# Layer 2's first product as a 2x2 block product with seven block products, its weight sums made in layer 1

## The chip, the cores and the metric

The kernel runs on one core of a Trainium2 chip. The metric is the device time of one execution in microseconds (us); lower is better. TensorE multiplies (PE in the profile, PEld its weight loads), VectorE (DVE) and ScalarE (ACT) work on elements, GpSimd (POOL) does little here, and SyncE (SP) issues the transfers.

## What is computed

An attention whose keys and values are averaged over groups of eight, then two feed-forward layers over the same 4608 tokens:

```python
k_p, v_p = k.reshape(B, H, Sp, 8, D).mean(axis=3), v.reshape(B, H, Sp, 8, D).mean(axis=3)
x = softmax(q @ k_p.T / sqrt(D)) @ v_p        # 4608 tokens x 512
h = x @ w_in;  x = (h - tanh(h)) @ w_out      # layer 1, 512 -> 2048 -> 512
h = x @ w_in2; x = (h * cos(h)) @ w_out2      # layer 2, the same sizes
```

All values are float32. The weights of both layers arrive as 64-bit numbers and are converted on the chip.

## The kernel before

The 4608 tokens are cut into 9 blocks of 512, the 2048 hidden columns into 16 tiles f of 128. TensorE works on tiles of type F32R, and each factor is kept as a high part and a low part (the rest after rounding), so one product is three matmuls: high by high, high by low, low by high. The attention of a later block runs between the steps of layer 1 on an earlier one.

A step (i, f) of layer 2 (the loop at the end of the kernel, lines 990 to 1008) has four stages:

- `emit_h2` (L763): 4 pieces of the inner dimension x 3 = 12 matmuls of 512 columns sum up h, a PSUM bank, with the weight tile `wi2[f]` loaded as the stationary side and the token block `xh`, `xl` streamed.
- `g2_a` (L773) on ACT finds the number of whole turns in h (L777, L778); DVE takes them away and clips (L780, L781, L782). `g2_b` (L785) takes the absolute value and the sine on ACT (L788, L789) and multiplies by h on DVE (L790).
- `g_second` (L597) splits the result into `gh` on ACT (L600) and `gl` on DVE (L601).
- `emit_out2` (L793): 4 x 3 = 12 matmuls of 512 columns add into the four banks `acc`, which stay open over the 16 steps of a block; `evac2` (L801) then copies them out and stores them.

All weight tiles of layer 2 stay in SBUF. They come in during block 8 of layer 1 (`w2_resident`, L734). The tokens of the next block are loaded and split one piece at a time (`x1_next`, L757). PSUM has eight banks: four `acc`, two for h, two for the attention (`att`).

The weights of layer 2 are converted in blocks 1 to 6 of layer 1: `converter` (L140) makes one float32 tile of a 64-bit one in three operations (L159 on ACT, L168 and L170 on DVE), then its high part on ACT (L174) and low part on DVE (L164) in one staging buffer `w2st`, which is stored to `s2i` or `s2o` (L677). The loop of layer 1 takes as many of its ticks after each step as a goal says (L981).

Up to block 7 of layer 1 a scheduler sets the order of the instructions on each engine. From block 8 on (`MANUAL = 8`) they stand in the order in which the code issues them. Each engine runs its own queue in order and waits on semaphores for the others.

Of the kernel before, what the change touches and what calls it, by code (L numbers as in the profile page):

```python
# [34 lines left out]
LOOK = 4  # L35


@with_exitstack
def fused_kernel(ctx: ExitStack, tc: tile.TileContext, q, k, v, w1i, w1o, w2i, w2o, out):
# [41 lines left out]
    xh = [cp.tile([128, RING], F32R, name=f"xh{c}") for c in range(KC)]  # L81
    xl = [cp.tile([128, RING], F32R, name=f"xl{c}") for c in range(KC)]
# [5 lines left out]
    s2i = [dram.tile([128, KC * 2 * 128], F32, name=f"s2i{f}") for f in range(NF)]  # L88
# [591 lines left out]
    w2_conv = converter(w2_pieces, w2_raw, w2_dest, lambda n: w2_load(n + 2), w2_fin, lambda n: True)  # L680
# [65 lines left out]
    def x1_load(i, c):
        xr = cp.tile([128, BLK], F32, tag="xe", name="xr", bufs=4)
        nc.sync.dma_start(out=xr, in_=x1s[i][:, c, :])
        xraw[i, c] = xr

    def x1_split(i, c):
        o = xoff(i)
        xr = xraw.pop((i, c))
        nc.scalar.activation(out=xh[c][:, o:o + BLK], in_=xr, func=AF.Copy)
        nc.vector.tensor_tensor(xl[c][:, o:o + BLK], xr, xh[c][:, o:o + BLK].bitcast(F32), op=ALU.subtract)

    def x1_next(i, f):  # L757
        if f % 3 == 0 and f > 0 and f <= 3 * KC:
            x1_load(i, f // 3 - 1)
        if f % 3 == 2 and f > 2 and f <= 3 * KC + 2:  # L760
            x1_split(i, f // 3 - 1)

    def emit_h2(wi, i):  # L763
        o = xoff(i)
        h = ps_h.tile([128, BLK], F32, tag="h", name="h")
        n = 0
        for c in range(KC):
            for wsel, xt in ((0, xh[c]), (0, xl[c]), (1, xh[c])):
                nc.tensor.matmul(out=h, lhsT=wi[:, c, wsel, :], rhs=xt[:, o:o + BLK], start=(n == 0), stop=(n == 3 * KC - 1))  # L769
                n += 1  # L770
        return h

    def g2_a(h, cols):  # L773
        kk = cp.tile([128, BLK], F32, tag="t0", name="kk", bufs=2)
        r = cp.tile([128, BLK], F32, tag="t1", name="r")
        for a, e in cols:
            nc.scalar.activation(out=kk[:, a:e], in_=h[:, a:e], func=AF.Identity, bias=bias_r, scale=INV_2PI)  # L777
            nc.scalar.activation(out=kk[:, a:e], in_=kk[:, a:e], func=AF.Copy, bias=-MAGIC)  # L778
        for a, e in cols:
            nc.vector.scalar_tensor_tensor(r[:, a:e], kk[:, a:e], -PI2_HI, h[:, a:e], op0=ALU.mult, op1=ALU.add)  # L780
            nc.vector.scalar_tensor_tensor(r[:, a:e], kk[:, a:e], -PI2_LO, r[:, a:e], op0=ALU.mult, op1=ALU.add)  # L781
            nc.vector.tensor_scalar(r[:, a:e], r[:, a:e], -PI_MAX, PI_MAX, op0=ALU.max, op1=ALU.min)  # L782
        return r

    def g2_b(h, r, cols):  # L785
        co = cp.tile([128, BLK], F32, tag="t4", name="co", bufs=2)
        for a, e in cols:
            nc.scalar.activation(out=r[:, a:e], in_=r[:, a:e], func=AF.Abs)  # L788
            nc.scalar.activation(out=co[:, a:e], in_=r[:, a:e], func=AF.Sin, bias=bias_c, scale=-1.0)  # L789
            nc.vector.tensor_tensor(co[:, a:e], co[:, a:e], h[:, a:e], op=ALU.mult)  # L790
        return co

    def emit_out2(wo, g, f):  # L793
        gh, gl = g
        for t in range(4):
            for n, (gt, wsel) in enumerate(((gh, 0), (gh, 1), (gl, 0))):
                nc.tensor.matmul(  # L797
                    out=acc[t], lhsT=gt[:, t * 128:(t + 1) * 128], rhs=wo[:, wsel, :],
                    start=(f == 0 and n == 0), stop=(f == NF - 1 and n == 2))
# [11 lines left out]
    if True:  # L811
# [178 lines left out]
        for i in range(NB):  # L990
            for f in range(NF):
                h = emit_h2(wi2[f], i)
                final = i == NB - 1 and f == NF - 1
                if final:
                    do_second()
# [45 lines left out]
```

## Time and profile before

| | us |
|---|---|
| median of 3 runs | 1763.99 (1760.97 to 1764.25) |
| profiled execution, its own time | 1759.05 |
| its span in the profile | 1757.2 |
| busy TensorE, DVE, ACT | 1727.4, 1291.0, 1160.6 |
| first and last h matmul of layer 2 start at | 962.9 and 1743.4 |

The span runs from the first to the last instruction of the profile. Busy times overlap, and each is a share of the whole span, over stages with different limits. The durations of matmuls overlap too, as one starts before the one ahead of it has ended; how fast they follow each other is read from their starts.

### The profile page before, as it was taken

To read this page: it belongs to the slowest core of one execution; us is meant where nothing else is said; L and a number is where in the kernel's file an instruction comes from. 1 tells how busy PE (TensorE), PEld (TensorE's weight loads), DVE (VectorE), ACT (ScalarE), POOL (GpSimd) and SP (SyncE) were. 2 spreads that over 40 slices of the span, in tenths; PEclk is the share of its full clock that TensorE was granted. 3 is DMA by queue.
4 is the path that set the end of the run, shared out by engine and by line. 5 is a ranking of instruction groups with operands and counts; after the bars stand their busy time and mean duration, and the time that the engine had idled before them with its cause. 6 is when DMAs were issued, how large, how long until landed. Compare 5 with 4: busy or idle time off the path is not lost.

```text
span 1757.2 us, 22513 instructions
## 1 busy us (share of the span) xinstructions
PE 1727.4 (98%) x7980; PEld 1421.3 (81%) x7980; DVE 1291.0 (73%) x2433; ACT 1160.6 (66%) x2081; POOL 13.8 (1%) x30
## 2 busy tenths in 40 slices
PE   6989999999999999999999999999999999999998
PEld 5767888888888888888888888888888888888887
DVE  7999999879889898877666566666666666656555
ACT  4777767677677777666565666666666666666665
POOL 2000000000000000000000000000000000000000
PEclk9999999999999999999999999999999999999999
DMA  7566756665565655423386201010101010101000
GB/s 245 192 211 210 238 179 207 196 194 181 163 207 179 202 173 163 141 78 120 130 302 208 92 1 48 1 49 1 49 0 49 1 49 0 49 1 48 1 25 24
DMA packets 116400, 202.27 MB, mean 115 GB/s; under 512 B 45376, under 2 KB 61760, under 8 KB 116288
## 3 DMA queue, kind: packets, MB, share of 16 engines
q1 hardware_dynamic: 112128, 199.79, 34.5%
q10 hardware_dynamic: 4160, 1.05, 0.3%
q8 instruction: 63, 1.03, 0.2%
q14 instruction: 49, 0.40, 0.1%
HBM read 156.76 MB, written 44.04 MB: 114 GB/s over the span
## 4 chain that ended last, share of the span: by engine, by line
PE 93%; DVE 2%; ACT 2%; DMA 1%; issue 1%; SPq 0%; ACTq 0%; DVEq 0%
PE h L769 22%; PE acc L797 22%; PE h L571 21%; PE acc L608 21%; PE att L414 2%; PE att L352 2%; PE att L381 1%; DMA raw<-in_moe_w_in_dram 1%; PE att L336 1%; DMA kv<-in_k_dram 1%; PE att L391 0%; ACT gh L600 0%; DVE w L594 0%; DMA raw<-in_moe_w_out_dram 0%; PE acc L414 0%
## 5 line engine op out<-in xcount | busy, mean ns | idle before, releaser
L769 PE MATMUL h<-xh,wi 128*128 128x512 f32 x1008 | 330.8, 389 | 0.0
L797 PE MATMUL acc<-wo,gh 128*128 128x512 f32 x1008 | 310.3, 389 | 0.0
L780 DVE SCALAR_TENSOR_TENSOR r<-kk,h 128x512 f32<-128x512 f32 (+1 forms) x145 | 99.2, 684 | 181.9 <-ACT kk L778 181.5
L797 PEld LDWEIGHTS acc<-wo,gh 128*128 128x128 f32 x1008 | 189.2, 188 | 39.2
L769 PEld LDWEIGHTS h<-xh,wi 128*128 128x128 f32 x1008 | 189.1, 188 | 39.2
L788 ACT ACTIVATE r<-r 128x512 f32<-128x512 f32 (+1 forms) x145 | 91.3, 630 | 194.9 <-DVE r L782 194.9
L571 PE MATMUL h<-xh,wi 128*128 128x512 f32 x576 | 196.5, 401 | 0.3 <-DVE wi L164 0.3
L769 PE MATMUL h<-xl,wi 128*128 128x512 f32 x504 | 196.1, 389 | 0.0
L797 PE MATMUL acc<-wo,gl 128*128 128x512 f32 x504 | 196.1, 389 | 0.0
L571 PE MATMUL h<-xh,ri 128*128 128x512 f32 x576 | 195.5, 399 | 0.0
L790 DVE TENSOR_TENSOR co<-co,h 128x512 f32<-128x512 f32 (+1 forms) x145 | 99.2, 684 | 117.7 <-ACT co L789 117.7
L608 PE MATMUL acc<-gh,wo 128*128 128x512 f32 x576 | 178.8, 393 | 6.1 <-ACT gh L600 6.1
L608 PE MATMUL acc<-gh,ro 128*128 128x512 f32 x576 | 178.3, 391 | 2.0 <-ACT gh L600 1.9
L589 DVE SCALAR_TENSOR_TENSOR w<-u,h 128x512 f32<-128x512 f32 x144 | 98.5, 684 | 97.6 <-ACT th L583 97.0
L777 ACT ACTIVATE kk<-h,bias_r 128x512 f32<-128x512 f32 (+1 forms) x145 | 99.5, 686 | 91.8 <-PE h L769 91.8
L582 ACT ACTIVATE u<-h 128x512 f32<-128x512 f32 x144 | 86.0, 597 | 92.3 <-PE h L571 91.0
L600 ACT ACTIVATE gh<-w 128x512 fp32r<-128x512 f32 x144 | 90.8, 631 | 62.7 <-DVE w L594 60.4
L608 PEld LDWEIGHTS acc<-gh,wo 128*128 128x128 f32 x576 | 107.8, 188 | 29.9 <-ACT gh L600 7.7
L608 PEld LDWEIGHTS acc<-gh,ro 128*128 128x128 f32 x576 | 107.6, 188 | 25.3 <-ACT gh L600 2.9
L571 PEld LDWEIGHTS h<-xh,wi 128*128 128x128 f32 x576 | 108.2, 189 | 22.6 <-DVE wi L164 0.7
L571 PEld LDWEIGHTS h<-xh,ri 128*128 128x128 f32 x576 | 108.2, 188 | 21.4 <-issue 0.2
L592 ACT ACTIVATE u<-u,bias_m 128x512 f32<-128x512 f32 x144 | 104.2, 724 | 30.8 <-DVE w L589 30.4
(178 smaller groups left out, 3340.8 us busy)
## 6 DMA issues: line engine op xcount, KB each, us to landing
ri<-s1i SPq DMA_DIRECT2D x64, 512.0 KB, 3.7
ro<-s1o SPq DMA_DIRECT2D x64, 512.0 KB, 3.6
raw<-in_moe_w_in_dram SPq DMA_DIRECT2D x32, 512.0 KB, 3.9
raw<-in_moe_w_out_dram SPq DMA_DIRECT2D x32, 512.0 KB, 3.5
x1s<-xe SPq DMA_DIRECT2D x36, 256.0 KB, 4.7
xr<-x1s SPq DMA_DIRECT2D x36, 256.0 KB, 4.0
out_dram<-xe SPq DMA_DIRECT2D x36, 256.0 KB, 2.0
kv<-in_k_dram SPq DMA_DIRECT2D x32, 256.0 KB, 3.8
```

The costliest lines, as they stand in the source:

```text
L571: nc.tensor.matmul(out=h[:, off:off + m], lhsT=wi[:, c, wsel, :], rhs=xt[:, r:r + m], start=(n == 0), stop=(n == 3 * KC - 1))
L582: nc.scalar.activation(out=u, in_=h, func=AF.Square)
L589: nc.vector.scalar_tensor_tensor(w, u, C2, h, op0=ALU.mult, op1=ALU.mult)
L592: nc.scalar.activation(out=u, in_=u, func=AF.Relu, bias=bias_m)
L600: nc.scalar.activation(out=gh[:, a:e], in_=w[:, a:e], func=AF.Copy)
L608: nc.tensor.matmul(out=acc[d], lhsT=wo[:, wsel, d * 128:(d + 1) * 128], rhs=gt, start=(f == 0 and n == 0), stop=(f == NF - 1 and n == 2))
L769: nc.tensor.matmul(out=h, lhsT=wi[:, c, wsel, :], rhs=xt[:, o:o + BLK], start=(n == 0), stop=(n == 3 * KC - 1))
L777: nc.scalar.activation(out=kk[:, a:e], in_=h[:, a:e], func=AF.Identity, bias=bias_r, scale=INV_2PI)
L780: nc.vector.scalar_tensor_tensor(r[:, a:e], kk[:, a:e], -PI2_HI, h[:, a:e], op0=ALU.mult, op1=ALU.add)
L788: nc.scalar.activation(out=r[:, a:e], in_=r[:, a:e], func=AF.Abs)
L790: nc.vector.tensor_tensor(co[:, a:e], co[:, a:e], h[:, a:e], op=ALU.mult)
L797: nc.tensor.matmul(out=acc[t], lhsT=gt[:, t * 128:(t + 1) * 128], rhs=wo[:, wsel, :], start=(f == 0 and n == 0), stop=(f == NF - 1 and n = ...
```

## The change

The first product of layer 2 now takes two weight tiles at a time, a pair j = f // 2, and is cut into 2x2 blocks: the inner dimension into two halves, the two tiles into one each, the 512 tokens into two halves of 256. Instead of eight block products there are seven (`product`, in the order `ORD`), each of 2 pieces x 3 = 6 matmuls of 256 columns: 42 per pair, where there were 24 of 512. Their factors are blocks or sums of blocks:

- The sums of weight blocks (four per pair of tiles) are made by the converter in layer 1 (`w2_converter`, which takes the place of `converter` there), with seven high and low parts per pair in place of the two tiles' own. `W2_TICKS` is 224 where there were 96 ticks.
- The sums of token blocks (four per token block, `sums`) and their high and low parts (seven, `fill_hi`, `fill_lo`) are made one token block ahead, spread over its 8 pairs by `WORK`. Twelve slots lie in the former `xh`, `xl`.
- The sums of the products (seven block sums) are made from PSUM: ACT copies product 1 (`hold`), DVE makes `join_a` (the first 256 tokens' two tiles, A) and `join_b` (the other half, B). Products 2 and 4 share one bank.

A and B are then handled as h was, 512 columns each, in the same operations (`turns`, `reduce`, `cosine`, `product_w`, `split`, `split_low`), and `unit` makes the second product, 12 matmuls of 512 columns each, for the two `acc` banks of its token half. A step of the loop in `second` holds the products of pair n, half A of pair n-1, and half B of pairs n-1 and n-2.

The block weights no longer stay in SBUF: for 7 of the 8 pairs their seven tiles of 256 KB are loaded anew for each token block into a ring of `WS = 18` slots (`load_slot`, one load behind each product, 441 in all); pair 7's stay. The tiles of the second product stay as before. Block 8 of layer 1 issues the first loads and the token sums of block 0 (`ahead`).

```diff
+ORD = (1, 2, 6, 7, 4, 5, 3)
...
-    w2_pieces = [(f, s) for f in range(NF) for s in range(2)]
+    w2_pieces = [(2 * j + e, s) for j in range(NF // 2) for s in range(2) for e in range(2)]
...
+    def w2_converter():
...
+            (a11, a12), (a21, a22) = [[x[:, 0:256], x[:, 256:512]] for x in (first, a)]
+            for src, sums_, ks in (
+                    (first, (), (0, 1)), (a, ((a21, a11, a21, ALU.subtract),), (3, 4)),
+                    (a, ((a21, a22, a21, ALU.subtract), (a22, a21, a11, ALU.add)), (2, 5)),
+                    (a12, ((a12, a12, a21, ALU.subtract),), (6,))):
+                for o, x, y, how in sums_:
+                    nc.vector.tensor_tensor(o, x, y, op=how)
+                    yield
+                m = len(ks)
+                st = ap.tile([128, 2, 2, 256], F32R, tag="w2st", name="w2st")
+                x = src.rearrange("p (e n) -> p e n", e=m)
+                nc.scalar.activation(out=st[:, 0:m, 0, :], in_=x, func=AF.Copy)
+                yield
+                nc.vector.tensor_tensor(st[:, 0:m, 1, :], x, st[:, 0:m, 0, :].bitcast(F32), op=ALU.subtract)
...
+    W2_TICKS = (NF // 2) * (4 * 3 + 2 * 2 + 4 * 2 + 4)
...
+    def sums(w):
+        o, x, y, how = {
+            1: ("t1", "12", "11", ALU.subtract), 3: ("12", "22", "12", ALU.subtract),
+            2: ("11", "12", "11", ALU.add), 4: ("t4", "21", "11", ALU.subtract)}[w]
+        nc.vector.tensor_tensor(raw_x(o), raw_x(x), raw_x(y), op=how)
...
+    WORK = {1: ((), (1,)), 2: ((), (3,)), 3: ((0,), (2,)), 4: ((1,), ()), 5: ((2,), (4,)), 6: ((3,), ()), 7: ((4, 5), ())}
...
+            t = two["bp"].tile([128, 2, 2, 128], F32R, tag="ws", name="ws", bufs=WS)
+            nc.sync.dma_start(out=t.rearrange("p w c n -> p (w c n)").bitcast(F32), in_=s2i[j][:, e, :])
...
+    def product(n, op, loads=1):
...
+        if op == 4:
+            out_ = g[24][:, 1, :]
         else:
+            if op in (2, 7, 3):
+                t = ps_a.tile([128, BLK], F32, tag="att", name="ab")
+            else:
+                t = ps_h.tile([128, BLK], F32, tag="h", name="ab")
...
+        for c in range(2):
+            for wsel, x in ((0, hi), (0, lo), (1, hi)):
+                nc.tensor.matmul(out=out_, lhsT=w[:, wsel, c, :], rhs=x[:, c], start=(m == 0), stop=(m == 5))
+                m += 1
+        if j != KEPT:
+            load_slot(loads)
...
+    def hold(n):
+        g = stage[n]
+        g["z"] = two["bp"].tile([128, 3, HN], F32, tag="z", name="z")
+        nc.scalar.activation(out=g["z"][:, 0, :], in_=g.pop(1), func=AF.Copy)
...
+    def join_a(n):
+        g = stage[n]
+        z = g["z"]
+        add(z[:, 2, :], g.pop(6), z[:, 0, :])
+        add(z[:, 1, :], g.pop(7), z[:, 2, :])
+        g["A"] = two["bp"].tile([128, 2, HN], F32, tag="hA", name="hA")
+        add(g["A"], g.pop(24), z[:, 0:2, :])
+
+    def join_b(n):
+        g = stage[n]
+        b = g["B"] = two["bp"].tile([128, 2, HN], F32, tag="hB", name="hB")
+        add(b, g.pop(5).unsqueeze(1).to_broadcast([128, 2, HN]), g.pop("z")[:, 1:3, :])
+        add(b[:, 1, :], g.pop(3), b[:, 1, :])
...
+    def unit(n, which):
+        gh, gl = stage[n].pop("g" + which)
+        j = n % NPAIR
+        for e in range(2):
+            f = 2 * j + (e if which == "A" else 1 - e)
+            for t in range(2):
+                o = e * HN + t * 128
+                for m, (gt, wsel) in enumerate(((gh, 0), (gh, 1), (gl, 0))):
+                    nc.tensor.matmul(
+                        out=acc[2 * "AB".index(which) + t], lhsT=gt[:, o:o + 128], rhs=wo2[f][:, wsel, :],
...
+            if live:
+                product(n, 1)
+                product(n, 2)
+            if both:
+                split(n - 2, "B")
+            if one:
+                reduce(n - 1, "A")
+                cosine(n - 1, "A")
+                join_b(n - 1)
+                turns(n - 1, "B")
+            if both:
+                split_low(n - 2, "B")
+                evac2(n - 2, "A")
+            if one:
+                product_w(n - 1, "A")
+            if live:
+                hold(n)
+            if one:
+                split(n - 1, "A")
...
+            if live:
+                product(n, 6)
+                product(n, 7)
+                product(n, 4)
+            if both:
+                unit(n - 2, "B")
+            if one:
+                reduce(n - 1, "B")
+                cosine(n - 1, "B")
+            if live:
+                join_a(n)
+                turns(n, "A")
+            if one:
+                split_low(n - 1, "A")
+                product_w(n - 1, "B")
...
+            if live:
+                product(n, 5)
+                product(n, 3)
+            if one:
+                unit(n - 1, "A")
...
-                    goal = (STEPS * len(w2_pieces) + 8) * ((i - 1) * NF + f + 1) // (NF * (NB - 3))
+                    goal = (W2_TICKS + 8) * ((i - 1) * NF + f + 1) // (NF * (NB - 3))
```

The first place is TensorE in the middle of layer 2, where the first product of a step meets the second. Before, the order is:

```order
L769 MATMUL h<-xh_77,wi 128x512
L769 MATMUL h<-xl_81,wi 128x512
L769 MATMUL h<-xh_77,wi 128x512
L797 MATMUL acc_82<-wo,gh 128x512 x2
L797 MATMUL acc_82<-wo,gl 128x512
L797 MATMUL acc_83<-wo,gh 128x512 x2
L797 MATMUL acc_83<-wo,gl 128x512
L797 MATMUL acc_84<-wo,gh 128x512 x2
L797 MATMUL acc_84<-wo,gl 128x512
```

With the change (`ab` is a bank of a block product, `ws` a slot of weights):

```order
L883 MATMUL ab<-xh,ws 128x256 x2
L883 MATMUL ab<-xl,ws 128x256
L883 MATMUL ab<-xh,ws 128x256
L954 MATMUL acc_76<-wo,gh 128x512 x2
L954 MATMUL acc_76<-wo,gl 128x512
L954 MATMUL acc_77<-wo,gh 128x512 x2
L954 MATMUL acc_77<-wo,gl 128x512
L954 MATMUL acc_76<-wo,gh 128x512 x2
L954 MATMUL acc_76<-wo,gl 128x512
L954 MATMUL acc_77<-wo,gh 128x512 x2
```

The h matmuls of 512 columns are block products of 256, and a group of the second product now fills two banks twice instead of four banks once.

The second place is DVE in layer 2, one step before:

```order
L780 SCALAR_TENSOR_TENSOR r<-kk,h 128x512
L781 SCALAR_TENSOR_TENSOR r<-kk,r 128x512
L782 TENSOR_SCALAR r<-r 128x512
L601 TENSOR_TENSOR gl<-co,gh 128x512
L790 TENSOR_TENSOR co<-co,h 128x512
```

and with the change most of one pair's step, from the sums of half B of the pair ahead to half B's product with h (L922 to L924 the reduction, L897 the sums of the products, L944 the low part, L935 the product with h):

```order
L897 TENSOR_TENSOR hB<-ab,z 128x512
L897 TENSOR_TENSOR hB<-ab,hB 128x256
L944 TENSOR_TENSOR gl<-w,gh 128x512
L935 TENSOR_TENSOR w<-r,hA 128x512
L922 SCALAR_TENSOR_TENSOR r<-kk,hB 128x512
L923 SCALAR_TENSOR_TENSOR r<-kk,r 128x512
L924 TENSOR_SCALAR r<-r 128x512
L897 TENSOR_TENSOR z<-ab,z 128x256 x2
L897 TENSOR_TENSOR hA<-ab,z 128x512
L944 TENSOR_TENSOR gl<-w,gh 128x512
L935 TENSOR_TENSOR w<-r,hB 128x512
```

The five operations of a step stand there for each half, and the sums of the products stand between them.

The third place is DVE in layer 1, at the end of a step, where the conversion's ticks are taken. Before:

```order
L591 SCALAR_TENSOR_TENSOR th<-th,h 128x512
L368 RECIPROCAL sm<-sm 96x8
L593 SCALAR_TENSOR_TENSOR w<-s,w 128x512
L369 TENSOR_TENSOR eb_155<-eb_155,sm 96x576
L594 COPY_PREDICATED w<-u,th 128x512
L168 TENSOR_SCALAR cva<-cva 128x512
```

With the change (L709 a low part of a weight block, L702 a sum of weight blocks):

```order
L594 SCALAR_TENSOR_TENSOR th<-th,h 128x512
L596 SCALAR_TENSOR_TENSOR w<-s,w 128x512
L597 COPY_PREDICATED w<-u,th 128x512
L709 TENSOR_TENSOR w2st<-cva,w2st 128x2x256
L424 TENSOR_TENSOR xl<-att,xh 128x256
L702 TENSOR_TENSOR cva<-cva 128x256
```

One operation of the conversion stood in such a place (L168), and two stand there now.

## Rows read from the trace of the kernel before

**Rows 1.** The page: busy us, share of the span and instructions of each engine.
```profile
PE 1727.4 (98%) x7980; PEld 1421.3 (81%) x7980; DVE 1291.0 (73%) x2433; ACT 1160.6 (66%) x2081; POOL 13.8 (1%) x30
```

**Rows 2.** Stretches: length, busy us (count) by engine, clock, DMA share, GB/s.
```profile
100.00:200.00 100.00, 95.84 (x448) 74.16 (x446) 94.14 (x206) 76.62 (x152) 1.41 (x2) 1.00 0.66 217
200.00:300.00 100.00, 99.68 (x505) 82.54 (x504) 96.69 (x223) 72.20 (x153) 0.00 (x0) 1.00 0.62 198
400.00:500.00 100.00, 100.00 (x494) 83.59 (x494) 88.96 (x182) 72.88 (x141) 0.00 (x0) 1.00 0.59 189
900.00:950.00 50.00, 50.00 (x222) 41.41 (x221) 32.14 (x49) 29.50 (x49) 0.00 (x0) 1.00 0.79 291
1300.00:1400.00 100.00, 100.00 (x443) 82.81 (x442) 61.41 (x100) 62.23 (x99) 0.00 (x0) 1.00 0.07 22
```

**Rows 3.** Timeline, layer 2: start, us, engine, line; first h matmul of two steps.
```profile
1300.22 0.39 PE L769 MATMUL h<-xh,wi 128*128 128x512 f32 x1
...
1311.10 0.39 PE L769 MATMUL h<-xh,wi 128*128 128x512 f32 x1
```

**Rows 4.** Timeline of the values product in layer 1: matmuls, then weight loads.
```profile
223.78 0.29 PE L414 MATMUL att<-ah,vbd 128*128 128x256 f32 x1
...
224.62 0.28 PE L414 MATMUL att<-ar,vbr 96*128 96x256 f32 x1
...
223.90 0.19 PEld L414 LDWEIGHTS att<-ah,vbd 128*128 128x128 f32 x1
224.02 0.19 PEld L414 LDWEIGHTS att<-ar,vbr 96*128 96x128 f32 x1
```

**Rows 5.** DVE groups by form: out<-in, shape, count; busy us, mean ns; idle before.
```profile
L781 DVE SCALAR_TENSOR_TENSOR r<-kk,r 128x512 f32<-128x512 f32 x143 | 99.1, 693 | 4.9
...
L790 DVE TENSOR_TENSOR co<-co,h 128x512 f32<-128x512 f32 x143 | 98.4, 688 | 117.0 <-ACT co L789 117.0
L780 DVE SCALAR_TENSOR_TENSOR r<-kk,h 128x512 f32<-128x512 f32 x143 | 98.4, 688 | 181.5 <-ACT kk L778 181.5
L601 DVE TENSOR_TENSOR gl<-co,gh 128x512 fp32r<-128x512 f32 x143 | 97.9, 685 | 0.7 <-ACT gh L600 0.7
...
L782 DVE TENSOR_SCALAR r<-r 128x512 f32<-128x512 f32 x143 | 61.3, 428 | 4.9
...
L755 DVE TENSOR_TENSOR xl<-xr,xh 128x512 fp32r<-128x512 f32 x36 | 24.6, 683 | 0.0
...
L421 DVE TENSOR_TENSOR xl<-att,xh 128x256 fp32r<-128x256 f32 x27 | 11.0, 419 | 2.0 <-ACT xh L417 2.0
```

**Rows 6.** Timeline of DVE in layer 2: four operations of two steps.
```profile
1300.53 0.43 DVE L782 TENSOR_SCALAR r<-r 128x512 f32<-128x512 f32 x1
1300.88 0.69 DVE L601 TENSOR_TENSOR gl<-co,gh 128x512 fp32r<-128x512 f32 x1
...
1304.53 0.69 DVE L780 SCALAR_TENSOR_TENSOR r<-kk,h 128x512 f32<-128x512 f32 x1 [1.42 <-ACT kk L778]
1305.25 0.69 DVE L781 SCALAR_TENSOR_TENSOR r<-kk,r 128x512 f32<-128x512 f32 x1
```

**Rows 7.** ACT groups by form in layer 2, columns as in rows 5.
```profile
L789 ACT ACTIVATE co<-r,bias_c 128x512 f32<-128x512 f32 x143 | 103.4, 723 | 4.7
L777 ACT ACTIVATE kk<-h,bias_r 128x512 f32<-128x512 f32 x143 | 98.5, 689 | 91.8 <-PE h L769 91.8
...
L788 ACT ACTIVATE r<-r 128x512 f32<-128x512 f32 x143 | 90.5, 633 | 194.0 <-DVE r L782 194.0
```

**Rows 8.** DMA issues: transfer, queue, count, size, median us to landing.
```profile
wi<-s2i SPq DMA_DIRECT2D x14, 512.0 KB, 6.7
```

**Rows 9.** Waits of TensorE, 100 to 200 us: us in total, times, longest.
```profile
PE acc L608 <- ACT gh L600: 3.6, 3, 1.3
```

**Rows 10.** Tile w2st: duration ns min/median/max, first and last start us, forms.
```profile
L174 ACT ACTIVATE w2st<-cva x32: 614/632/677, 182.8 to 738.9; 128x512 fp32r<-128x512 f32 x32
L164 DVE TENSOR_TENSOR w2st<-cva,w2st x32: 668/678/701, 192.0 to 744.4; 128x512 fp32r<-128x512 f32 x32
```

More of the change, by code (lines that the diff above doesn't have):

```diff
@@ L746, in x1_load @@
[L746 to L773, printed above, removed]
-        kk = cp.tile([128, BLK], F32, tag="t0", name="kk", bufs=2)
[L775 to L799, printed above, removed]
@@ L801, in evac2, with xslot, raw_x @@
-    def evac2(i):
-        for t in range(4):
+    wo2 = {}
+    HN = BLK // 2
+    NPAIR = NF // 2
+    STEPS2 = NB * NPAIR
+    WS = 18
+    NQ = len(ORD)
+    NX = 12
+    KEPT = NPAIR - 1
+    two = {}
+    def xslot(k):
+        k %= NX
+        c0, o = 2 * (k % 2), HN * (k // 2)
+        return [t[:, c0:c0 + 2, o:o + HN] for t in (xh_t, xl_t)]
+    def raw_x(m):
+        if m in ("t1", "t4"):
+            return two[m]
+        c0, o = 2 * (int(m[0]) - 1), HN * (int(m[1]) - 1)
+        return two["xr"][:, c0:c0 + 2, o:o + HN]
@@ new lines, in fill_hi, with fill_lo, fill @@
+    def fill_hi(i, k):
+        nc.scalar.activation(out=xslot(i * NQ + k)[0], in_=raw_x(SOURCE[ORD[k]]), func=AF.Copy)
+    def fill_lo(i, k):
+        hi, lo = xslot(i * NQ + k)
+        nc.vector.tensor_tensor(lo, raw_x(SOURCE[ORD[k]]), hi.bitcast(F32), op=ALU.subtract)
+    def fill(i, k):
+        fill_hi(i, k)
+        fill_lo(i, k)
+    WORK = {1: ((), (1,)), 2: ((), (3,)), 3: ((0,), (2,)), 4: ((1,), ()), 5: ((2,), (4,)), 6: ((3,), ()), 7: ((4, 5), ())}
+    slots, kept = {}, {}
+    to_load = [(i, j, e) for i in range(NB) for j in range(NPAIR) for e in range(NQ) if j != KEPT]
@@ new lines, in load_out, with open_second @@
+    def load_out(m):
+        f = RES[m]
+        for e, tag in enumerate((f"wi{f}", f"wo{f}")):
+            wo2[2 * m + e] = cp.tile([128, 2, DM], F32R, tag=tag, name="wo")
+            nc.sync.dma_start(out=rows(wo2[2 * m + e]), in_=s2o[2 * m + e])
+    def open_second(pool):
+        two["bp"] = pool
+        two["xr"] = pool.tile([128, KC, BLK], F32, tag="xr", name="xr")
+        two["t1"] = pool.tile([128, 2, HN], F32, tag="x1", name="x1")
+        two["t4"] = pool.tile([128, 2, HN], F32, tag="x4", name="x4")
@@ new lines, in second @@
+    def second():
+        load_x(1)
+        product(0, 1)
+        hold(0)
+        product(0, 2)
+        do_out(1)
+        do_second()
+        product(0, 6)
+        product(0, 7)
+        product(0, 4)
+        join_a(0)
+        turns(0, "A")
+        do_out(1)
+        product(0, 5)
+        product(0, 3)
+        load_out(NPAIR - 2)
+        load_out(NPAIR - 1)
+        load_kept()
+        for n in range(1, STEPS2 + 3):
+            i, j = divmod(n, NPAIR)
+            live, one, both = n < STEPS2, n <= STEPS2, 2 <= n <= STEPS2 + 1
+            more = live and i + 1 < NB
+            if live:
[17 more added lines that the diff above has]
+                split(n - 1, "A")
+            fills, adds = WORK.get(j, ((), ())) if more else ((), ())
+            for k in fills:
+                fill_hi(i + 1, k)
+            if live and i and j == 0:
+                fill_hi(i, 6)
+            if live:
[13 more added lines that the diff above has]
+                product_w(n - 1, "B")
+            if both:
+                evac2(n - 2, "B")
+            for k in fills:
+                fill_lo(i + 1, k)
+            for w in adds:
+                sums(w)
+            if live and i and j == 0:
+                fill_lo(i, 6)
+            if more and j == 0:
+                load_x(i + 1)
+            if live:
[3 more added lines that the diff above has]
+                unit(n - 1, "A")
@@ L986, in fused_kernel @@
                 else:
[L987 to L1011 removed]
+                    ahead(f)
+        second()
 _INS = ['q', 'k', 'v', 'moe_w_in', 'moe_w_out', 'moe2_w_in', 'moe2_w_out']
```

176 lines of the change are left out of this document (120 added, 56 removed).

## The prediction

> **What bounds the kernel now.** I read the page's first section, then the stretches by stage, then one step of layer 2 in order of time. The page says that TensorE is busy 98% of the span, and VectorE 73% [rows 1]. The stretches say where [rows 2]: in layer 2 (1300 to 1400 us) TensorE is busy all 100 us while VectorE (DVE) has 61 and ScalarE (ACT) 62; in layer 1 (400 to 500 us) TensorE has 100 again, but DVE has 89. So layer 2 is bound by TensorE alone with a third of DVE free, and layer 1 is bound by TensorE with DVE close behind. A busy TensorE is not TensorE at its peak, so I take its pace from the starts of its matmuls, not from their durations. One step of layer 2 (12 matmuls into h, 12 into acc, all of 512 columns) starts at 1300.22, the next but one at 1311.10 [rows 3]: 48 matmuls in 10.88 us, 0.2267 us each. There are 144 steps, 72 pairs of 10.88 us.
>
> **TensorE in layer 2, the term that the change is for.** Per pair 24 matmuls of 512 columns into h become 42 of 256 columns: 10752 columns in place of 12288. The 24 of the second product stay. Whether half the columns take half the time decides, for each matmul loads its own weights. The values product of layer 1 shows it, from tiles of the same type (F32R in the code): eight matmuls of 256 columns, each with a load of its own, start between 223.78 and 224.62 [rows 4], 0.84/7 = 0.120 us apart, though one load lasts 0.19 us: loads overlap each other and the matmuls. So a pair takes 42 x 0.120 + 24 x 0.2267 = 5.04 + 5.44 = 10.48 us, 0.40 us less, and 72 pairs 28.9 us less. The stamps are rounded to 0.01 us, so 0.120 may be 0.0014 off either way; over 42 x 72 matmuls this is 4.3 us: 24.6 to 33.1.
>
> A rule of the Trainium skill speaks against it: the page "TensorE: Matmul & The Clock Gate", Part 3 (Packing small matmuls), says that a weight load overlaps running matmuls only where the two use different row groups, and here both use all 128 rows. The trace disagrees: the weight loads at 223.90 and 224.02 both start within the 0.29 us of the full-height matmul of 223.78 [rows 4]. I go by the rows; what the rule would give is the third rival.
>
> **VectorE in layer 2, the term that could spoil it.** Before, a pair has two rounds of five operations of 512 columns [rows 5]: 2 x (0.688 + 0.693 + 0.428 + 0.688 + 0.685) = 6.36 us. They stay. New are the sums of the seven products: three of 256 columns at 0.419 (the nearest row of that size also reads PSUM) and two of 512 at 0.688, 2.63 us. Once per token block (8 pairs) come 7 low parts in place of 4 and 4 token sums, 11 x 0.684, and two copies at about the same 0.684: 8.9/8 = 1.11 us per pair. The sum is 10.10 us against TensorE's 10.48, so the spare third is gone, and what counts is how far DVE's own waits reach. (a) An operation that does not need the one before it starts early: 1300.88 against an end of 1300.96 [rows 6], 0.08 us. Of 15 operations in a pair some 8 stand so: 0.7 us back. (b) One that does need it starts late: from 1304.53 to 1305.25 for 0.69 [rows 6], 0.03 each, 0.2 us. (c) Round trips through ACT [rows 7]. Block half A: from the last sum to its first reduction ACT needs 0.689 + 0.633 = 1.32 (its second pass is of the size of the third row); the queue has gl and w between, 1.37 less 0.16, so about 0.1 shows. Half B: after the reduction of A, ACT does 0.633 + 0.723 for A and 1.32 for B, 2.68; DVE has in that time two sums, gl and w, 2.48 less 0.16, so about 0.4 shows. The two waits for the sine (1.36) have 1.5 us or more of other DVE work under them. So DVE's own period is 10.10 - 0.7 + 0.2 + 0.5 = 10.1 us: shorter than 10.48 by only 0.4. I cost the sums at nothing, because the matmuls of the same pair hide them; without that cover they would cost what DVE exceeds 10.48 by, 72 times. TensorE's waits for DVE have cover too: before product 3 can take a buffer, the last sum of half A must be done, and a half of the second product (12 x 0.2267 = 2.72) and product 5 (0.72) stand between on TensorE, against that one sum. ACT gains one copy of 256 columns a pair and three fills a block; at 62 of 100 it has room.
>
> **Transfers.** Seven of eight pairs now load 7 x 262 KB = 1.84 MB in 10.48 us, 175 GB/s; before, layer 2 moved 22, while 291 GB/s went through at 900 to 950 us with TensorE's pace unchanged [rows 2]. In that burst 512 KB landed after 6.7 us [rows 8], and 18 slots reach 18/7 x 10.48 = 27 us ahead. On SP's queue a load waits for the product that frees its slot, and behind it stand only later loads, the next tokens and the stores, none due within 10 us. Zero.
>
> **Entry into layer 2.** In step 1 no earlier pair is there whose second product could fill TensorE while the first half goes through sums, reduction, sine and split. One half is missing, 2.7 us at most; I take all of it. At the end the last sums are covered by three halves (8.2 us) of the pairs before; nothing. Block 8 gets 3 low parts and 4 sums more (4.8 us of DVE in some 90 us at 64 of 100 [rows 2]): nothing.
>
> **Layer 1.** Per pair of weight tiles DVE gets four sums of 256 columns (1.68) and low parts of 3 x 0.684 + 0.419 in place of 2 x 0.684 (1.10): 2.78, and 8 pairs 22.2 us. ACT gets at most 8 x 2 x 0.63 = 10 us. The conversion runs from 183 to 744 us [rows 10], so DVE rises by 4.0 of 100, from 89 to 93. The bounds are 0 and 22.2 (all of it on TensorE's path). Rows on both sides: at 94.1 TensorE lost 4.2 of 100, most of it 3.6 us of waits for gh [rows 2, 9]; at 96.7 it lost 0.3. The second is nearer to the stretch concerned, the first stands at the entry of the kernel. I take 0.7 of 100 over 560 us: 4 us. The six stores of one staging buffer per pair of tiles, in place of four, wait on each other; ACT may stand there, and that is in the 4.
>
> **The sum.** Against the profiled execution (span 1757.2, its own time 1759.05): 1759.05 - 28.9 + 2.7 + 4 = 1736.9. The median of the runs shown is 4.9 above that execution, so by it 1763.99 - 22.2 = 1741.8: I predict **1742 us**.
>
> **The rivals.**
> First, DVE becomes the bound in layer 2, and the kernel is slower. The place is the DVE queue of each pair. DVE's period is 10.10 - 0.7 + 0.2 = 9.6 us plus the waits that show. From 0.9 us of them it passes 10.48 and eats the gain; from 1.2 on the kernel is slower (9.6 + 1.2 is the old 10.88 less the 6.7 us of entry and layer 1 spread over 72 pairs). If one of the two waits for the sine shows in full beside the 0.5 above, the period is 9.6 + 0.5 + 1.36 = 11.5 us: 72 x (11.5 - 10.88) = +45, with entry and layer 1 1763.99 + 45 + 6.7 = 1816 us. For it: an engine at 96% in strict order between two others that it waits for. Against: each wait has named work under it. Chance 0.10.
> Second, layer 1 pays the gain back: all 22.2 us on the path, 1763.99 - 28.9 + 2.7 + 22.2 = 1760, no change that can be told. For it: DVE at 89 to 97 there. Against: 96.7 with TensorE idle for 0.3 [rows 2]. Chance 0.08.
> Third, weight loads do not overlap when columns are few: 0.19 for the load [rows 4] and 0.2267 - 0.120 = 0.107 for the stream of 256 columns, 0.295 us each, 42 x 0.295 = 12.4 us in place of 5.44 for the old 24, + 6.95 x 72 = +500: 2264 us. Rows 4 exclude it nearly: 0.01. This is where the page's rule would lead, and by it the trace disagrees.
> Fourth, the change does not do what it says, in that the streamed weights come late: the first loads share the queue with the last of layer 1, and two landings of 6.7 us [rows 8] lie bare at the entry, 13 us: 1755. Chance 0.02.
>
> **How the numbers follow.** The forecast has 0.79. Told from no change is a shift over 0.2%, 3.5 us. Faster: the forecast and the fourth, 0.81; same: the second, 0.08; slower: the first and the third, 0.11. The range goes from 1763.99 - 33.1 + 1 (the best pace, layer 1 and entry almost free) = 1732 to 1758 (20 us lost in layer 1, nearly the second rival).
>
> **What would show it.** Right: matmuls of the blocks 0.12 us apart, a pair 10.4 to 10.6 us, TensorE busy all 100 us of a middle stretch with DVE near 90; DVE's idle time put down to products; layer 2 some 26 us shorter; layer 1 longer by a few us. Wrong: a pair over 10.7 us with TensorE waiting for DVE sums or low parts (first rival); layer 1 over 10 us longer (second); starts over 0.13 us apart (third); TensorE waiting for DMA (fourth).

## The result, and the profile after

| | before | with the change |
|---|---|---|
| median, runs on the same chip | 1764.12 us (1760.97 to 1765.38, 4 runs) | 1735.62 us (1735.33 to 1738.40, 4 runs) |
| ratio, 95% interval | | 0.9845 [0.9828, 0.9862] |
| profiled execution, span | 1759.05, 1757.2 | 1738.40, 1736.6 |

The kernel became 28.5 us faster by the medians and 20.6 us faster from profiled execution to profiled execution. The profiled execution of before was the fastest of its kind and that of the change is the slowest of its four. A second profiled execution of the changed kernel (experiment 9) took 1734.68 us with a span of 1732.9, 24.3 less than before.

The page after: busy us, share of the span and instructions of each engine, which answers to [rows 1]:

```profile
PE 1705.5 (98%) x9276; PEld 1461.7 (84%) x9276; DVE 1507.5 (87%) x2899; ACT 1202.3 (69%) x2191; POOL 13.9 (1%) x30
```

The stretches after, columns as in [rows 2]:

```profile
200.00:300.00 100.00, 100.00 (x507) 82.52 (x506) 96.39 (x223) 73.06 (x152) 0.00 (x0) 1.00 0.68 211
400.00:500.00 100.00, 100.00 (x495) 83.64 (x494) 89.90 (x190) 72.10 (x140) 0.00 (x0) 1.00 0.59 189
980.00:990.00 10.00, 8.10 (x39) 6.64 (x40) 9.07 (x17) 6.76 (x13) 0.00 (x0) 0.83 1.02 391
1300.00:1400.00 100.00, 100.00 (x630) 90.67 (x629) 90.04 (x160) 69.33 (x116) 0.00 (x0) 1.00 0.55 179
```

TensorE is still busy for all of a middle stretch of layer 2. It now does 630 matmuls there in place of 443, and DVE has gone from 61 to 90 of 100. The 10 us after 980 hold the only waits of TensorE in layer 2 (listed below).

The pace of TensorE is read from its starts (timeline after, PE): the first products of a step, and then the first product of the kept pair in block 0 and in block 7 (seven blocks, 56 pairs, later).

```profile
1303.85 0.28 PE L883 MATMUL ab<-xh,ws 128*128 128x256 f32 x1
1303.96 0.28 PE L883 MATMUL ab<-xl,ws 128*128 128x256 f32 x1
1304.08 0.40 PE L883 MATMUL ab<-xh,ws 128*128 128x256 f32 x2
1304.32 0.28 PE L883 MATMUL ab<-xl,ws 128*128 128x256 f32 x1
...
1307.44 0.63 PE L954 MATMUL acc<-wo,gh 128*128 128x512 f32 x2
1307.91 0.39 PE L954 MATMUL acc<-wo,gl 128*128 128x512 f32 x1
```

```profile
1040.85 0.28 PE L883 MATMUL ab<-xh,wk 128*128 128x256 f32 x1
...
1629.97 0.28 PE L883 MATMUL ab<-xh,wk 128*128 128x256 f32 x1
```

Thirty matmuls of 256 columns take 1307.44 - 1303.85 = 3.59 us, 0.120 each, and a pair takes (1629.97 - 1040.85)/56 = 10.52 us. Before it was 10.88 [rows 3].

One step of DVE (timeline after):

```profile
1304.75 0.69 DVE L922 SCALAR_TENSOR_TENSOR r<-kk,hB 128x512 f32<-128x512 f32 x1 [0.41 <-ACT kk L916]
1305.47 0.69 DVE L923 SCALAR_TENSOR_TENSOR r<-kk,r 128x512 f32<-128x512 f32 x1
1306.20 0.43 DVE L924 TENSOR_SCALAR r<-r 128x512 f32<-128x512 f32 x1
1306.54 0.94 DVE L897 TENSOR_TENSOR z<-ab,z 128x256 f32<-128x256 f32 x2
1307.65 0.69 DVE L897 TENSOR_TENSOR hA<-ab,z 128x512 f32<-128x512 f32 x1 [0.16 <-PE ab L883]
1308.25 0.68 DVE L944 TENSOR_TENSOR gl<-w,gh 128x512 fp32r<-128x512 f32 x1
1308.85 0.69 DVE L935 TENSOR_TENSOR w<-r,hB 128x512 f32<-128x512 f32 x1
```

An operation that does not need the one ahead starts 0.60 us after it (1308.25, 1308.85), one that does 0.72 (1304.75, 1305.47). The wait for ACT in half B shows with 0.41 us; none of the waits for the sine shows.

All waits of TensorE from 960 us to the end, as the view of waits gives them (us in total, times, longest):

```profile
PE ab L883 <- DVE z L897: 1.5, 1, 1.5
PE ab L883 <- ACT z L894: 0.6, 1, 0.6
```

**Where the time went.** From the first h matmul of layer 2 to the end of the span before took 1757.2 - 962.9 = 794.3 us; with the change 1736.6 - 965.5 = 771.1, and 1732.9 - 963.4 = 769.5 in the second profiled execution. The pace gives 72 x (10.88 - 10.52) = 25.9 us back. The two ends of layer 2, its first pairs and its last, take 2.7 of it again in the first execution and 1.1 in the second. Layer 2 begins 2.6 us later in the first, 0.5 in the second.

The entry (timeline after, PE and DVE), in the second pair of weight tiles:

```profile
980.37 0.39 PE L883 MATMUL ab<-xh,ws 128*128 128x256 f32 x1 [0.59 <-ACT z L894]
...
981.88 0.95 DVE L897 TENSOR_TENSOR z<-ab,z 128x256 f32<-128x256 f32 x2
...
982.88 0.38 PE L883 MATMUL ab<-xh,ws 128*128 128x256 f32 x1 [1.53 <-DVE z L897]
...
983.69 0.63 PE L954 MATMUL acc<-wo,gh 128*128 128x512 f32 x2
...
988.26 0.28 PE L883 MATMUL ab<-xh,ws 128*128 128x256 f32 x1
```

A product waits 1.53 us for the sums that free its bank. DVE makes them late, because the reduction of half B ahead of them in its queue came late from ACT, which did this first:

```profile
974.06 2.04 ACT L618 ACTIVATE xe<-acc 128x512 f32<-128x512 f32 x4
976.10 0.63 ACT L929 ACTIVATE r<-r 128x512 f32<-128x512 f32 x1
976.75 1.28 ACT L930 ACT_TABLE_LOAD   x1
978.05 0.72 ACT L930 ACTIVATE r<-r,bias_c 128x512 f32<-128x512 f32 x1
```

Those are four copies out of layer 1's banks and the table of the sine. After the wait the granted clock fell (stretches after, columns as in [rows 2]):

```profile
981.00:983.00 2.00, 0.47 (x4) 0.27 (x4) 1.76 (x5) 0.97 (x2) 0.00 (x0) 1.00 1.00 359
983.00:985.00 2.00, 2.00 (x10) 1.49 (x11) 2.00 (x4) 1.69 (x4) 0.00 (x0) 0.91 1.04 412
985.00:987.00 2.00, 2.00 (x6) 1.59 (x5) 1.93 (x4) 0.56 (x2) 0.00 (x0) 0.50 1.00 406
987.00:989.00 2.00, 2.00 (x11) 1.66 (x11) 1.90 (x5) 1.72 (x3) 0.00 (x0) 0.74 1.03 420
```

The twelve matmuls from 983.69 took 4.57 us to 988.26, against 2.75 for twelve such at the full clock: 1.8 us lost to a granted clock of 0.50 (1.2 GHz), on top of the 2.1 us of waiting. In the second profiled execution the same two waits stand there and the clock stayed at 1.00; its distance from the first to the last h matmul is 754.7 us in place of 756.3. Experiments 3, 5 and 6 have the same two waits too, and the clock stayed at 1.00 in them.

### The profile page after: what moved, and what is told of

It reads as the page before. It is cut to its first block, busy times and chain, and to the rows that moved or that the text cites. A ratio compares the mean times of both kernels' runs of the same rounds, so it can differ in the third digit from the quotient of the medians.

```text
span 1736.6 us, 27131 instructions
## 1 busy us (share of the span) xinstructions
PE 1705.5 (98%) x9276; PEld 1461.7 (84%) x9276; DVE 1507.5 (87%) x2899; ACT 1202.3 (69%) x2191; POOL 13.9 (1%) x30
## 4 chain that ended last, share of the span: by engine, by line
PE 90%; DVE 4%; ACT 3%; DMA 2%; issue 1%; SPq 0%; ACTq 0%; DVEq 0%
PE acc L954 23%; PE ab L883 21%; PE h L574 20%; PE acc L611 19%; PE att L417 2%; PE att L355 2%; DMA raw<-in_moe_w_in_dram 1%; PE att L384 1%; PE att L339 1%; DVE w L592 0%; DMA s2i<-w2st 0%; DVE w L596 0%; ACT u L585 0%; ACT u L595 0%; DMA raw<-in_moe_w_out_dram 0%
## 5 line engine op out<-in xcount | busy, mean ns | idle before, releaser
L954 PE MATMUL acc<-wo,gh 128*128 128x512 f32 x1152 | 359.4, 393 | 0.0
L883 PE MATMUL ab<-xh,ws 128*128 128x256 f32 x1764 | 337.5, 283 | 2.1 <-DVE z L897 1.5
L883 PEld LDWEIGHTS ab<-xh,ws 128*128 128x128 f32 x1764 | 283.4, 191 | 7.5 <-DVE z L897 1.7
L883 PE MATMUL ab<-xl,ws 128*128 128x256 f32 x882 | 249.5, 283 | 0.0
L929 ACT ACTIVATE r<-r 128x512 f32<-128x512 f32 x144 | 91.0, 632 | 163.4 <-DVE r L924 162.2
L574 PE MATMUL h<-xh,wi 128*128 128x512 f32 x576 | 196.8, 401 | 1.3 <-ACT wi L177 1.3
L883 PEld LDWEIGHTS ab<-xl,ws 128*128 128x128 f32 x882 | 168.8, 191 | 4.9
L954 PEld LDWEIGHTS acc<-wo,gl 128*128 128x128 f32 x576 | 108.6, 189 | 24.1 <-DVE gl L944 0.4
L574 PEld LDWEIGHTS h<-xh,wi 128*128 128x128 f32 x576 | 108.5, 189 | 23.9 <-ACT wi L177 2.0
L597 DVE COPY_PREDICATED w<-u,th 128x512 f32<-128x512 uint32 x144 | 108.5, 754 | 9.1 <-ACT u L595 1.3
```

What stands on the lines that cost most here:

```text
L574: nc.tensor.matmul(out=h[:, off:off + m], lhsT=wi[:, c, wsel, :], rhs=xt[:, r:r + m], start=(n == 0), stop=(n == 3 * KC - 1))
L597: step_end[0] = nc.vector.copy_predicated(w, u.bitcast(U32), th)
L883: nc.tensor.matmul(out=out_, lhsT=w[:, wsel, c, :], rhs=x[:, c], start=(m == 0), stop=(m == 5))
L929: nc.scalar.activation(out=r, in_=r, func=AF.Abs)
L954: nc.tensor.matmul(out=acc[2 * "AB".index(which) + t], lhsT=gt[:, o:o + 128], rhs=wo2[f][:, wsel, :], start=(j == 0 and e == 0 and m == 0) ...
```

## The experiments

The theory: TensorE alone bounds layer 2, DVE's added work lies beside it with a small margin, and transfers and weight sums cost nothing. The rivals are those of the prediction.

**1. Narrow matmuls alone, the kernel before.** It computes the same with as many columns.

```diff
-            for wsel, xt in ((0, xh[c]), (0, xl[c]), (1, xh[c])):
-                nc.tensor.matmul(out=h, lhsT=wi[:, c, wsel, :], rhs=xt[:, o:o + BLK], ...
+        for a in (0, BLK // 2):
+            ...
+                    nc.tensor.matmul(out=h[:, a:a + BLK // 2], lhsT=wi[:, c, wsel, :], rhs=xt[:, o + a:o + a + BLK // 2], ...
```

> The kernel before, its layer 2 h product in two groups of 12 matmuls of 256 columns in place of 12 of 512. Theory (a matmul costs 0.4167 ns a column plus 13 ns, whatever its weight load): a step grows from 12 x 0.2267 = 2.72 us to 24 x 0.120 = 2.88, +0.16 x 144 = +23 us on the kernel before (1787). Rival 1 (a weight load does not overlap): 24 x 0.295 = 7.1 us a step, +630 us. Rival 2 (only columns count): 0 us.

Measured: 1785.45 us against 1761.83, ratio 1.0133 [1.0112, 1.0153], +23.6 us. The middle stretch of its profile:

```profile
1300.00:1400.00 100.00, 100.00 (x641) 91.17 (x640) 59.41 (x97) 60.46 (x97) 0.00 (x0) 1.00 0.07 22
```

It follows that a matmul of 256 columns is a little dearer than half of one of 512: 23.6 us over 144 x 12 matmuls that became two each is 0.0137 us for each split. The trace puts it a little higher in all, at 26 us from the first to the last h matmul (806.4 against 780.4), 0.18 a step, and tells where it lies: the twelve matmuls of the second product, though not changed, take 2.75 us behind the narrow ones (1300.26 to 1303.01), 0.03 more than the 2.72 before, and the other 0.15 are 0.013 for each split. That TensorE then does 641 matmuls in 100 us excludes weight loads that stand bare.

**2 to 4. The margin of DVE.** Experiment 2 leaves out the three sums of 256 columns; the two sums of 512 stay and read product 1's copy where they read those sums. Experiments 3 and 4 keep all and add one and two unused DVE operations of 512 columns per pair, behind the product of half A.

```diff
-        add(z[:, 2, :], g.pop(6), z[:, 0, :])
-        add(z[:, 1, :], g.pop(7), z[:, 2, :])
...
-        add(b[:, 1, :], g.pop(3), b[:, 1, :])
```

```diff
                 product_w(n - 1, "A")
+                for _ in range(1):
+                    nc.vector.tensor_tensor(two["dy"], two["dx"], two["dx"], op=ALU.add)
```

Experiment 4 has `range(2)` there.

> The changed kernel without the three block sums of 256 columns a pair (products 6, 7 and 3 are computed but not added), 1.26 us of DVE less a pair of 10.48. Theory (the matmuls hide the sums, DVE is idle for 1.0 us a pair): a pair stays at 10.48 us, TensorE 100 of 100 in a middle stretch, DVE falls from 90 to about 79; only the entry into layer 2 shortens, 0 to 2.5 us in all. Rival (DVE helps to set the pace of a pair): over 10 us less.

> The changed kernel with one more DVE operation of 512 columns on tiles of its own in each pair (0.60 us of the queue, 72 times 43 us). Theory (DVE is idle for 1.0 us in a pair of 10.48): it fits, 0 to 3 us longer, DVE at about 96. Rival (no slack: DVE's idle time is all forced waits): +20 to +43 us.

> The same with two such operations, 1.2 us a pair. Theory: more than the 1.0 us that is idle, so DVE becomes the bound: +0.2 to +0.6 us a pair, +14 to +43 us, TensorE waiting for DVE sums. Rival (slack larger than it looks, as waits move): under 5 us. Rival (no slack): +60 to +86 us.

Measured, all beside a before of 1761.83 us: 1737.84 us (0.9860 [0.9845, 0.9874]) without the sums, 1737.42 (0.9861 [0.9839, 0.9884]) with one more operation, 1781.26 (1.0109 [1.0088, 1.0129]) with two. The middle stretch of experiments 2, 3 and 4, in this order:

```profile
1300.00:1400.00 100.00, 100.00 (x629) 90.67 (x629) 79.51 (x131) 68.89 (x116) 0.00 (x0) 1.00 0.56 179
```

```profile
1300.00:1400.00 100.00, 100.00 (x630) 90.68 (x629) 94.34 (x168) 69.49 (x116) 0.00 (x0) 1.00 0.56 180
```

```profile
1300.00:1400.00 100.00, 97.06 (x594) 85.70 (x593) 95.22 (x169) 64.79 (x109) 0.00 (x0) 1.00 0.53 169
```

and the longest waits of TensorE in layer 2 in experiment 4:

```profile
PE ab L887 <- DVE xl L808: 17.6, 8, 2.2
PE ab L887 <- DVE hB L901: 2.9, 15, 0.2
```

Taking DVE from 90 to 80 of 100 gives nothing, and taking it to 94 costs nothing; the next operation costs 44 us, just over the 43 that its theory allowed. So the sums lie wholly beside TensorE, and the rival of DVE as the bound is real but two operations away. In experiment 2 the entry changes: its products wait no more, but a matmul of the second product waits 1.6 us for a low part there, and the distance from the first to the last h matmul is 753.9 us.

The price gives DVE's own period, as a mean over the pairs: from the first to the last h matmul experiment 4 takes 797.5 us and experiment 3 755.0, 42.5/71 = 0.60 more per pair, so 10.52 + 0.60 = 11.12 us with two operations of 0.60 in it, and about 9.9 without. Experiment 3 stands at 9.9 + 0.6 = 10.5, just at the edge.

The pairs of a token block do not share this evenly. Two stretches between two block borders of experiment 4, and then the 3 us behind the wait at each of these borders:

```profile
1068.20:1110.00 41.80, 41.80 (x263) 37.58 (x263) 38.67 (x68) 26.17 (x45) 0.00 (x0) 1.00 0.62 198
1110.50:1155.00 44.50, 41.93 (x256) 36.67 (x255) 42.56 (x76) 29.55 (x50) 0.00 (x0) 1.00 0.43 132
1065.00:1068.00 3.00, 3.00 (x11) 2.51 (x11) 2.83 (x6) 1.55 (x3) 0.00 (x0) 0.50 0.70 224
1155.00:1158.00 3.00, 3.00 (x16) 2.59 (x17) 2.83 (x6) 1.38 (x3) 0.00 (x0) 1.00 0.65 175
```

In the first pairs of a block TensorE loses nothing even with two more operations; in the later ones DVE falls behind, and at the first pair of the next block a product waits up to 2.2 us for the last low part of the tokens. The waits listed are 20.5 of the 42.5 us. Behind four of the eight waits of 2.2 us the granted clock also fell to 0.50 (third row; 1.2 GHz, 11 matmuls in 3 us), behind the other four it did not (fourth row, 16 matmuls). The rest are short waits in the later pairs, which were not added up. Part of the price is thus the clock's, so 9.9 is if anything too high for DVE's own period.

**5. No stream of weights.** From pair 2 on the products take the kept tiles and no block weights are loaded; the loads of the kept tiles stand ahead of two others that they followed before (`load_kept`, not shown).

```diff
-        w = kept[k] if j == KEPT else slots.pop((i, j, k))
+        w = kept[k] if n > 1 else slots.pop((i, j, k))
...
-        if j != KEPT:
-            load_slot(loads)
```

> The changed kernel without the 423 loads of block weights after the first 18: from pair 2 on every pair uses the tiles of pair 7 (so the products of the other pairs are of the wrong weights). Theory (the loads are hidden: 256 KB land in 3.5 us, 18 slots reach 27 us ahead): a pair stays at 10.48 us, no change beyond 2 us. Rival (the traffic slows operations or the entry): over 5 us less.

Measured: 1738.31 us against 1761.62, 0.9867 [0.9847, 0.9887], no difference from the changed kernel that can be told; the distance from the first to the last h matmul is 754.7 us, as in the second profile of the changed kernel. The 423 loads left out cost nothing. The waits at the entry stay (1.5 and 0.6 us). Whether crowded transfers have a part in them is not shown, since other loads still fill that stretch (359 GB/s at 980 to 990, against 391 with the change).

**6. No weight sums in layer 1.** The converter skips the four sums per pair of tiles.

```diff
-                for o, x, y, how in sums_:
-                    nc.vector.tensor_tensor(o, x, y, op=how)
-                    yield
```

> The changed kernel without the 32 weight sums in layer 1 (the products are of unsummed blocks), 13.4 us of DVE less between 183 and 750 us, the same stores. Theory (layer 1 loses nothing to the conversion; it started layer 2 2.6 us later only because TensorE's clock was low for part of 100 to 200 us in the execution that was profiled): layer 2 starts within 1 us of the changed kernel's start once the lost clock is taken off, no change beyond 1 us. Rival (my forecast of 4 us for all DVE work added there): 2 to 3 us less.

Measured: 1739.88 us against 1761.62, 0.9874 [0.9856, 0.9892]; layer 2 begins at 968.2 us, later than in either profile of the changed kernel itself (965.5, 963.4). The sums, 13.4 of the 22.2 us of DVE work that were forecast for layer 1, cost nothing that can be told. Layer 2's start varies for another reason, the first 150 us: experiment 1 has layer 1 as before and begins layer 2 at 965.8, before at 962.9. The stretch that differs, before and then experiment 1:

```profile
100.00:150.00 50.00, 45.97 (x211) 34.15 (x209) 47.40 (x94) 38.85 (x75) 0.00 (x0) 1.00 0.59 195
```

```profile
100.00:150.00 50.00, 46.26 (x201) 34.94 (x199) 45.35 (x89) 36.63 (x70) 0.00 (x0) 0.94 0.56 188
```

**7 and 8. The entry.** Experiment 7 loads the sine's table early, behind layer 1's last split. Experiment 8 does so too and moves half of layer 1's last second product behind product 4 of pair 1, with its copies.

```diff
         do_second()
+        early = two["bp"].tile([128, 1], F32, tag="early", name="early")
+        nc.scalar.activation(out=early, in_=bias_c, func=AF.Sin)
...
-        do_out(1)
+        _, f1, wo1, g1 = pend.pop(0)
+        emit_out1(wo1, g1, f1, (0, 1))
+        evac1(NB - 1, (0, 1))
...
                 unit(n - 2, "B")
+            if n == 1:
+                emit_out1(wo1, g1, f1, (2, 3))
+                load_kept()
...
+            if n == 1:
+                evac1(NB - 1, (2, 3))
```

> The changed kernel with one sine of a single column issued on ACT right after layer 1's last split, so that the table load (1.28 us) falls in ACT's idle time and not in the chain of pair 0. Theory (at the entry product 3 of pair 1 waits for sums that stand on DVE behind a reduction that waits for that chain): the wait of 1.5 us for the sums shrinks to 0.3 to 1, and if TensorE's clock then stays up, 1.9 us more: 1 to 4 us less. Rival (the entry waits for the sums of pair 0 for another reason): no change.

> The same early sine, and half of the last second product of layer 1 (6 of 12 matmuls) moved behind product 4 of pair 1, where the second product of an earlier pair stands in later steps. Theory (the entry lacks one half's cover): TensorE's idle time at the entry falls from 2.4 us to about 1.5, in pieces under 0.8 us, its clock stays at the upper level, 2 to 4 us less. Rival (the missing cover only moves, from pair 1 to pair 0): the same idle time, no change.

Measured, against 1761.62: 1739.55 us (0.9875 [0.9857, 0.9893]) and 1736.75 (0.9854 [0.9832, 0.9875]). In the traces TensorE's waits at the entry fell from 2.1 us (the 2.4 in experiment 8's expectation stands in no view) to 1.1 us in experiment 7, one wait, for the sums, where 0.3 to 1 was expected, and in 8 to these:

```profile
PE ab L883 <- DVE hB L897: 0.5, 1, 0.5
PE ab L883 <- DVE z L897: 0.4, 1, 0.4
```

The distance from the first to the last h matmul is 753.4 us in both, against 756.3 in the changed kernel's first profile, which has the stretch of low clock. The medians do not show the 1 to 4 and 2 to 4 us that were expected, and no run of the changed kernel stands beside them on that chip. So the two kernels were set side by side.

**9 and 10. The changed kernel and that of experiment 8 on one chip, five rounds.**

> The changed kernel itself, run beside e10_entry_same_chip on one chip. The theory that the wait at layer 2's entry is lost time: this one has the entry waits 1.5 + 0.6 us and a distance of 755 to 757 us from the first to the last h matmul of layer 2, and its median stands 1.5 to 3 us above that of e10. Rival, that the wait at the entry is made up for elsewhere: the medians agree within 1 us and the distances too.

> The kernel of e8_entry once more (early sine, and half of layer 1's last second product behind product 4 of the first pair), beside e9_changed_same_chip on one chip. The theory that the wait at layer 2's entry is lost time: entry waits under 1 us, 753 to 754 us from the first to the last h matmul, and a median 1.5 to 3 us below that of e9. Rival, that the wait is made up for elsewhere: medians within 1 us of each other.

Measured: 1737.21 us (1734.68 to 1743.03; 0.9864 [0.9841, 0.9888]) and 1736.38 us (1732.74 to 1739.03; 0.9847 [0.9828, 0.9867]), against 1764.14. First and last h matmul, of experiment 9 and then 10 (duration min/median/max, first and last start):

```profile
L883 PE MATMUL ab<-xh,ws x1764: 277/283/387, 963.4 to 1707.5; 128*128 128x256 f32 x196
...
L883 PE MATMUL ab<-xh,wk x252: 277/283/283, 1037.1 to 1718.1; 128*128 128x256 f32 x126
```

```profile
L883 PE MATMUL ab<-xh,ws x1764: 277/283/386, 969.0 to 1711.9; 128*128 128x256 f32 x196
...
L883 PE MATMUL ab<-xh,wk x252: 277/283/283, 1041.5 to 1722.4; 128*128 128x256 f32 x126
```

The distances are 754.7 and 753.4 us: 1.3 apart, about the 1.2 us that the waits differ by (2.1 against 0.9). Experiments 5 and 6, with 2.1 us of waits, measure 754.7 too, and experiments 7 and 8 753.4. So the waits are lost time, but less of it than the 1.5 to 3 us expected, and the medians, 0.8 apart with runs that spread over 6 to 8 us, cannot show it. No version is shown to beat the changed kernel.

## Why the prediction was right

**The forecast** was 1742 us, 22.2 below the median, by TensorE's pace in layer 2; measured was 28.5 below. Most of the signs named for it came: 0.12 us a matmul, 10.52 a pair, TensorE busy for all of a middle stretch with DVE at 90. Three did not come as said. Layer 2 is 23.2 to 24.8 us shorter where 26 was said; of DVE's waits between 990 and 1720 us 21 us are put down to products, but 26 to ACT, the wait of half B; and layer 1 did not grow longer (below).

**The pace.** Predicted were 0.120 us a matmul, 10.48 a pair and 28.9 us in all (72 x 0.40 is 28.8). The 0.120 is right to the last digit. A pair takes 10.52, and the term gives 25.9. That lies inside the bounds, but by luck, for these allowed only for the rounding of the stamps and not for what the working left out, the change of shape: a half of the second product takes 2.75 us from its first start to the next product's (1301.10 to 1303.85), where 12 x 0.2267 is 2.72, twice per pair. Experiment 1 has the same 2.75 with the second product as before, so it comes with the narrow matmuls ahead. It also prices the halving itself, at the 0.013 us that 2 x 0.120 - 0.2267 said.

**The weight loads** overlap, as [rows 4] had it: experiment 1 and the 630 matmuls in 100 us leave no room for the third rival. By the rule of the Trainium skill ("TensorE: Matmul & The Clock Gate", Part 3, Packing small matmuls) the loads would have stood bare, since all use the same rows; the trace disagrees, with starts 0.12 us apart. One of the two loads of [rows 4] was of 96 rows only; those of the block products are all of 128.

**DVE.** Predicted were 10.1 us of its own per pair, a margin of 0.4 and no cost. Experiments 3 and 4 put the period at 9.9 and the margin at 0.6, as means over a token block: one more operation is free, two are not. The wait of 0.4 us for half B is in the trace as 0.41. The first rival exists, 1.2 us of added work away: there the time is 1781 us, slower than before, and the longest waits stand at the borders of token blocks, which the prediction did not look at.

**Transfers** cost zero, as said: without the loads experiment 5 is no shorter, and no wait of TensorE in layer 2 is for a transfer. This closes the fourth rival.

**The entry** got 2.7 us for a missing half. The waits do stand right behind the place that lacks it, behind product 4 of the second pair. But they are 2.1 us, plus 1.8 us of low clock in the first execution, and the end of the kernel gives about 1 us back (from the start of the last matmul to the end of the span 5.2 us before, 4.0 after). The ends together took 2.7 and 1.1 us, so that the first figure is the one forecast is luck. How long the waits are depends on when ACT and DVE are done: with the sine's table moved away 1.1 us of them are left, with half of the four copies and half of layer 1's last second product moved as well 0.9. The prediction named neither the table nor the copies. What a whole half in that place would have hidden was not measured.

**Layer 1** got 4 us of its 22.2. Layer 2 begins 2.6 and 0.5 us later in the two profiles of the changed kernel, but this was lost before the conversion begins. The first h matmul of layer 1's second block, before, after and in the second profile (timelines, PE):

```profile
161.77 0.39 PE L571 MATMUL h<-xh,wi 128*128 128x512 f32 x1
```

```profile
164.63 0.39 PE L574 MATMUL h<-xh,wi 128*128 128x512 f32 x1
```

```profile
162.82 0.39 PE L574 MATMUL h<-xh,wi 128*128 128x512 f32 x1
```

From there to the start of layer 2 (962.94, 965.51 and 963.37) it takes 801.2 us before and 800.9 and 800.5 with the change. The other profiles with the changed layer 1 lie between 800.1 and 801.9, and experiment 6, without the sums, at 803.7. So the added work cost nothing there. The stretch from 200 to 960 us, before and then after:

```profile
200.00:960.00 760.00, 758.82 (x3671) 630.87 (x3670) 629.56 (x1252) 525.21 (x1001) 0.00 (x0) 1.00 0.55 179
```

```profile
200.00:960.00 760.00, 759.00 (x3673) 630.63 (x3672) 649.61 (x1312) 533.52 (x1022) 0.00 (x0) 1.00 0.56 185
```

DVE's work there rose by 20.0 us, near the 22.2 worked out, and TensorE stays busy for 759 of 760: all of it found room. The price of 4 us was too high by all of it, since the 4.2 of 100 that TensorE lost at the kernel's entry [rows 2], which raised it, did not come with DVE's load in this stretch, and the second rival, 22 us, is excluded.

**The sum.** Against the profiled execution it was 1736.9 us; 1738.4 and 1734.68 were measured. The mechanism held, but that the sum came so near is luck: the errors of pace (3.0 too hopeful) and of layer 1 (4 too cautious) nearly cancel, and the later start of layer 2 (0.5 and 2.6 us) came from the first 160 us of the kernel, which no term had. Set upon the median the forecast became 6 us too high, because the profiled execution of before lay 5 us below its median and that of the change did not.

## What to carry to other kernels

When an engine works in strict order beside the bounding one, its margin is found by adding unused operations one at a time until the time moves, which here told some 0.6 us a pair where the busy share alone did not tell what the next operation would cost: 94 of 100 was free, 95 cost 44 us. A product cut into fewer and narrower matmuls pays by what a narrow one costs from start to start, and such matmuls elsewhere in the same trace give that before anything is built. Look at the first steps of a new stage by themselves: the steady order that hides everything does not stand there yet.

## What was not expected of the hardware

The granted clock fell to 0.50 (1.2 GHz) at 985 to 987 us, behind waits of 0.59 and 1.53 us of TensorE, in one execution, and stayed at 1.00 in four others with the same waits (experiments 3, 5, 6 and 9). In experiment 4 it fell behind four of eight waits of 2.2 us. In the first 150 us of the kernel such falls come in other places in each execution: at 100 to 150 us the clock was 1.00 before, 0.93 in the first profile of the change and 0.98 in the second. The start of layer 2 varied from 962.9 to 965.8 us with the same layer 1, and experiment 10, with 0.86 in the first 50 us, began it at 969.0 where experiment 8, the same kernel at 0.97, began it at 963.6. Differences of this size between the kernels' times were therefore not read as effects of an edit.
